# Linear attention block on one core: moving the first loads between two queues, cutting the crossbar transfer finer, and waiting for every store at the end

## The chip, the cores and the metric

The kernel runs on 1 core of one Trainium2 chip. The metric is device microseconds of one execution. Times of the kernel before: 99.91, 99.98 and 100.34 us, so a median of 99.98 us. The profiled execution is one of its own, 100.18 us in all, of which the profile covers a span of 98.5 us.

A core has five instruction streams. PE multiplies matrices (PEld is its weight load), DVE and ACT work elementwise, POOL is used for constants here, and SP issues transfers. Transfers are issued from SP and ACT in this kernel; each of the two feeds a queue of its own, q1 for SP and q10 for ACT in the profile, and both queues are worked off by the same 16 DMA engines.

## The reference

```
x (1, 2048, 640), wqkv (640, 1920), wo (640, 640), all bf16; 32 heads of 20 columns
qkv = x @ wqkv                      # q, k, v
phi(t) = where(t > 0, t + 1, exp(t)) + 1e-6
pq, pk = phi(q), phi(k)
kv  = sum over s of pk[s, d] * v[s, e]     # per head, 20 x 20
z   = sum over s of pk[s, d]
num = pq @ kv ;  den = pq . z + 1e-6
out = (num / den) @ wo
```

The sequence has 2048 rows, which the kernel walks in 16 tiles of 128 rows.

## The kernel before

The program is written out by hand for each engine. A small class `Plan` records every operation with what it reads and writes, and works out which semaphores it must wait for (`add`, lines 36 to 76); `emit` then writes each engine's list in the recorded order. Every DMA has a semaphore of its own. An engine's `known` table holds the semaphore values that its earlier waits imply, so that a wait which is implied already is left out.

**Stages.** First come the keys. For each of the 16 row tiles, ten matmuls (five blocks of 128 of the contraction, two halves of 320 columns) compute x @ Wk into two PSUM banks (`k_half`, L293); ACT and DVE then make phi of it (`k_phi`, L306 to L311). After that PE runs the x-by-phi(k) products (L317), the query tiles (L354), small products for kv and the folded output weights (L445, L472), the denominators (L544), and the output (L576), whose tiles are stored row tile by row tile. The order of these is spelled out in one string.

**How x gets to PE.** A matmul needs x transposed, in the buffer `xT`. For row tiles 2 to 15 the transposed form is fetched by transposing transfers on SP (`load_xT`, L189), here called the crossbar transfers; the list `XCH` says which rows each of them covers. Tiles 0 and 1 (`NPE = 2`) are loaded plain into `xn`, transposed by PE against an identity (`transpose_x`, L200), and copied from PSUM to `xT`: part 0, blocks 0 and 1, by DVE (L212), part 1, blocks 2 to 4, by ACT (L209). `xn_keys` names what a transposition has to wait for.

**The loads at the head** (`load_wk`). SP issues the left half of x tile 0, then blocks 0, 2 and 3 of Wk, then the five crossbar transfers, and then `load_rest`: the query weights, the remaining plain x tiles, and the other weights. ACT issues the right half of x tile 0, x tile 1, and blocks 1 and 4 of Wk. A block of Wk is 128 rows of 640 columns, 160 KB, as much as one tile of x.

**PE at the head** (L625 to L636). Before the data is there PE runs dummy matmuls on constants (`warm`, L283): five of 512 columns and one of 128. Then it transposes tile 0, runs one more dummy matmul of 512 columns, and follows this list, in which `k` stands for key matmuls (row tile, block of the contraction, and with a letter only one of the two halves) and `t` for a transposition of tile 1:

```
order = "k00a t1a k00b t1b k10 k01 k11 k02 k12 k03 k13 k04 k14"
```

**The end** (L730 to L734). After all engines' lists SP waits for the output stores. A store is skipped there if SP's `known` table says that an earlier wait implies it.

Of the kernel before, what the change touches and what calls it, by code (L numbers as in the profile page):

```python
# [84 lines left out]
def bass_standalone__linear_attn_block__prompt_kernel(nc, x, wqkv, wo, out):  # L85
# [5 lines left out]
    HALF = D // 2  # L91
# [9 lines left out]
    with contextlib.ExitStack() as ctx:  # L101
        es = ctx.enter_context

        def sb(name, cols, dt=BF16):
            return es(nc.sbuf_tensor(name, [128, cols], dt))

        xT = sb("xT", NC_ * S)
        xn = sb("xn", NT * D)
# [23 lines left out]
        ident = sb("ident", 128)  # L132
# [7 lines left out]
        P = Plan(nc, es)  # L140

        def bank(b, n=BK, off=0, parts=128):
            return ps[0:parts, BK * b + off:BK * b + off + n]
# [9 lines left out]
        def pool_const():  # L153
# [21 lines left out]
            for t in range(2):  # L175
# [3 lines left out]

        NPE = 2  # L180
        XCH = [(0, 128), (128, 256),
               (256, 384), (384, 640), (640, 1024), (1024, 1536), (1536, 2048)]

        def xch_of(row):
            return next(i for i, (a, b) in enumerate(XCH) if a <= row < b)
# [7 lines left out]
        def transpose_x(st, part):  # L193
            lo, hi = ((0, 2), (2, NC_))[part]
            b = (6, 4)[st] + part
            v = bank(b, HALF).bitcast(BF16)

            def mm(e):
                for c in range(lo, hi):
                    r = e.transpose(  # L200
                        v[:, 128 * c:128 * c + 128],
                        xn[:, st * D + 128 * c:st * D + 128 * c + 128], ident[:, :])
                return r
            P.add("pe", mm, reads=xn_keys(st)[:1 + part] + ["ident"], writes=[("bank", b)])
            dst = xT[:, :].rearrange("p (c s) -> p c s", s=S)[
                :, lo:hi, 128 * st:128 * st + 128]
            src = v.rearrange("p (c s) -> p c s", s=128)[:, lo:hi, :]
            if part:
                P.add("act", lambda e: e.copy(dst, src),  # L209
                      reads=[("bank", b), "table"], writes=[("xT", st, lo)])  # L210
            else:
                P.add("dve", lambda e: e.tensor_copy(dst, src),  # L212
                      reads=[("bank", b)], writes=[("xT", st, lo)])
# [15 lines left out]
        def load_xn(a, b, eng):  # L229
            P.add(eng, lambda e: e.dma_start(  # L230
                xn[:, a * D:b * D].rearrange("p (t n) -> p t n", n=D),
                x[0, 128 * a:128 * b, :].rearrange("(t p) n -> p t n", p=128)),
                writes=[("xn", t) for t in range(a, b)], dma=True)

        def load_wk():
            tl = mybir.InstLoadActFuncSet(
                name=nc.get_next_instruction_name(),
                act_func_set_id=ACT_TABLE_SET_LN_EXP, ins=[], outs=[])
            P.add("act", lambda e: e.add_instruction(tl), writes=["table"])
            for eng, lo in (("sp", 0), ("act", HALF)):  # L240
                P.add(eng, lambda e, lo=lo: e.dma_start(  # L241
                    xn[:, lo:lo + HALF], x[0, 0:128, lo:lo + HALF]),
                    writes=[("xn", 0, lo)], dma=True)
            for eng, what in (("sp", "w01 w23 w34"), ("act", "x12 w12 w45")):
                for k in what.split():
                    a, b = int(k[1]), int(k[2])
                    if k[0] == "x":
                        load_xn(a, b, eng)
                    else:
                        P.add(eng, lambda e, a=a, b=b: e.dma_start(  # L250
                            wk[:, a * D:b * D].rearrange("p (c n) -> p c n", n=D),
                            wqkv[128 * a:128 * b, D:2 * D].rearrange("(c p) n -> p c n", p=128)),
                            writes=[("wk", c) for c in range(a, b)], dma=True)

        def xn_keys(t):
            return [("xn", t)] if t else [("xn", 0, 0), ("xn", 0, HALF)]

        def load_rest():
            w_cols(wqn, 0, D, 0, "wqn", "sp")
# [21 lines left out]
        def warm(n, cols=BK):  # L281
            for _ in range(n):
                P.add("pe", lambda e: e.matmul(  # L283
                    bank(4, cols), nc.const_aps.tensor(1.0, [128, 128], BF16),
                    nc.const_aps.tensor(1.0, [128, cols], BF16), start=True, stop=True),
                    writes=[("bank", 4)])
# [37 lines left out]
        def p_step(h, st, ds=range(NC_)):  # L324

            def mm(e):
                for d in ds:
                    r = state_mm(e, h, d, st)
                return r
            P.add("pe", mm, reads=xn_keys(st) + [("pk", st)],  # L330
                  writes=sorted({("bank", d // PB[h]) for d in ds}))
# [288 lines left out]

        pool_const()
        load_wk()
        load_xT()
        load_rest()
        warm(5)  # L625
        warm(1, 128)
        for part in range(2):
            transpose_x(0, part)
        warm(1)
        order = "k00a t1a k00b t1b k10 k01 k11 k02 k12 k03 k13 k04 k14"  # L630
        for k in order.split():
            st, part = int(k[1]), "ab".find(k[-1])
            if k[0] == "t":
                transpose_x(st, part)
            else:
                for h in range(2) if part < 0 else (part,):  # L636
                    k_half(st, h, (int(k[2]),))
# [41 lines left out]
        def p_block(h, ds):  # L679
            def mm(e):  # L680
                for d in ds:
                    for st in range(NB, NT):
                        r = state_mm(e, h, d, st)
                return r
            P.add("pe", mm, reads=[k for st in range(NB, NT) for k in xn_keys(st) + [("pk", st)]],
                  writes=[("bank", ds[0] // PB[h])])
            p_out(h, ds)
            if ds[-1] == NC_ - 1:
                small.extend((0, 1) if h else (2, 3, 4))
# [39 lines left out]
            P.emit(name, eng)  # L729
        for key in out_keys:  # L730
            op = P.writers[key]
            if P.known["sp"].get(op.sem, 0) >= op.val:
                continue
            nc.sync.wait_ge(P.sem_obj[op.sem], op.val)  # L734


# [26 lines left out]
```

## Time and profile before

| | |
|---|---|
| median of 3 runs | 99.98 us (99.91 to 100.34) |
| profiled execution | 100.18 us, span 98.5 us |
| PE busy | 97% of the span, 699 matmuls |
| DVE, ACT, POOL busy | 65%, 50%, 5% |
| first key matmul | 4.37 us after the span's start |
| first key matmul of row tile 2 | 7.9 us |
| last matmul's copy out of PSUM starts | 96.5 us |

Of each transfer at the head, the issue and the moment when all of it had landed (us from the start of the span):

| queue | transfer | issued | landed |
|---|---|---|---|
| SP | x tile 0, left half, 80 KB | 0.79 | 2.86 |
| SP | Wk block 0, 160 KB | 1.24 | 4.32 |
| SP | Wk block 2 | 1.70 | 5.18 |
| SP | Wk block 3 | 2.17 | 6.03 |
| ACT | x tile 0, right half, 80 KB | 0.82 | 3.03 |
| ACT | x tile 1, 160 KB | 1.24 | 4.51 |
| ACT | Wk block 1 | 1.72 | 5.36 |
| ACT | Wk block 4 | 2.21 | 6.23 |
| SP | crossbar, rows 256 to 384 | 2.65 | 7.02 |
| SP | crossbar, rows 384 to 640 | 4.03 | 9.02 |
| SP | crossbar, rows 640 to 1024 | 6.29 | 12.11 |
| SP | crossbar, rows 1024 to 1536 | 8.04 | 16.11 |
| SP | crossbar, rows 1536 to 2048 | 12.63 | 18.23 |

The profile's chain of work that ended last is followed back from the last instruction: where an instruction waited, the chain steps to what released it, and otherwise to the instruction before it on the same engine. The length of a piece is the time that it adds to the span. A matmul's duration in the profile is modelled and overlaps with the next one's; how far apart matmuls *start* is what a row of them costs.

### The profile page before, as it was taken

What the parts mean: (1) busy time and instruction counts of PE and PEld (TensorE: products, weight loads), DVE (VectorE), ACT (ScalarE), POOL (GpSimd) and SP (SyncE); (2) the same over time, 40 slices, a digit from 0 to 9 for tenths busy, and PEclk for the clock granted to TensorE, in tenths of its full rate; (3) what the DMA queues carried; (4) which work ended last, traced back from release to release, by engine and by line L of the source; (5) the groups of instructions that cost most, each with busy time, mean ns of one, the idle gap of its engine ahead of it and who ended that gap; (6) DMA issues with size and microseconds to landing.
All of it is one profiled execution on the core that took longest, in us unless ns stands there. A gap on an engine that the chain in (4) does not pass through costs nothing.

```text
span 98.5 us, 1813 instructions
## 1 busy us (share of the span) xinstructions
PE 95.4 (97%) x699; PEld 61.1 (62%) x699; DVE 63.7 (65%) x124; ACT 48.8 (50%) x93; POOL 4.7 (5%) x19
## 2 busy tenths in 40 slices
PE   6999999999999999999999999999999999999991
PEld 2567677777755454445587867655557677777771
DVE  5315988988899529997829836758999207272122
ACT  5116455544526220005806466796988765453532
POOL 6400000000000000000000420000000000000000
DMA  2999999999999177000250023313200335632334
GB/s 69 310 258 164 148 222 187 248 379 370 338 163 136 14 169 166 0 0 0 57 83 7 0 61 92 96 29 87 82 0 0 133 72 156 212 122 88 130 133 133
DMA packets 26367, 12.59 MB, mean 128 GB/s; under 512 B 18552, under 2 KB 26360, under 8 KB 26360
## 3 DMA queue, kind: packets, MB, share of 16 engines
q1 hardware_dynamic: 25640, 11.87, 50.3%
q10 hardware_dynamic: 720, 0.61, 1.9%
q8 instruction: 5, 0.08, 0.3%
q14 instruction: 2, 0.02, 0.1%
HBM read 5.90 MB, written 2.62 MB: 87 GB/s over the span
## 4 chain that ended last, share of the span: by engine, by line
PE 93%; DMA 3%; SPq 0%; issue 0%; ACT 0%
PE ps L293 23%; PE ps L576 22%; PE ps L317 22%; PE ps L354 22%; DMA wk<-in_wqkv_dram 3%; PE ps L445 1%; PE ps L544 1%; PE ps L472 1%; SPq L241 0%; PE ps L200 0%; ACT osb L599 0%
## 5 line engine op out<-in xcount | busy, mean ns | idle before, releaser
L317 PE MATMUL ps<-pk,xn 128*128 128x480 bf16 (+1 forms) x160 | 23.2, 299 | 0.0
L354 PE MATMUL ps<-xT,wqn 128*128 128x512 bf16 x100 | 23.1, 379 | 0.0
L293 PE MATMUL ps<-wk,xT 128*128 128x320 bf16 x160 | 22.6, 301 | 0.3 <-DMA wk<-in_wqkv_dram 0.2
L576 PE MATMUL ps<-w2p,pq 128*128 128x320 bf16 (+2 forms) x170 | 22.1, 291 | 0.0
L293 PEld LDWEIGHTS ps<-wk,xT 128*128 128x128 bf16 x160 | 15.5, 98 | 7.2 <-DMA wk<-in_wqkv_dram 0.8
L576 PEld LDWEIGHTS ps<-w2p,pq 128*128 128x128 bf16 x170 | 15.9, 98 | 6.2 <-issue 0.2
L317 PEld LDWEIGHTS ps<-pk,xn 128*128 128x128 bf16 x160 | 13.6, 98 | 9.4 <-issue 0.3
L362 ACT ACTIVATE eq<-ps 128x512 bf16<-128x512 f32 x20 | 11.9, 597 | 13.8 <-PE ps L354 13.6
L354 PEld LDWEIGHTS ps<-xT,wqn 128*128 128x128 bf16 x100 | 11.5, 118 | 9.1 <-issue 0.3
L306 ACT ACTIVATE ek<-ps 128x640 bf16<-128x640 f32 x16 | 11.2, 704 | 11.0 <-PE ps L293 10.3
L599 ACT CAST osb<-ps 128x320 bf16<-128x320 f32 (+2 forms) x27 | 11.0, 413 | 9.7 <-PE ps L576 8.8
L311 DVE SCALAR_TENSOR_TENSOR pk<-ps,ek 128x640 bf16<-128x640 f32 x16 | 13.2, 825 | 0.6
L569 DVE TENSOR_TENSOR pq<-pq,rd 128x512 bf16<-128x512 bf16 x20 | 7.3, 418 | 4.3 <-DMA rd<-rdc 4.3
L375 DVE TENSOR_SCALAR eq<-eq 128x512 bf16<-128x512 bf16 x20 | 5.7, 287 | 5.9 <-ACT eq L362 5.8
L602 DVE CAST osb<-ps 128x320 bf16<-128x320 f32 (+1 forms) x7 | 3.2, 455 | 8.7 <-PE ps L576 8.7
L308 DVE TENSOR_SCALAR ek<-ek 128x640 bf16<-128x640 bf16 x16 | 5.2, 325 | 5.3 <-ACT ek L306 5.3
L366 ACT ACTIVATE rq<-ps 128x512 bf16<-128x512 f32 x13 | 7.7, 592 | 0.0
L339 ACT CAST pt<-ps 128x480 bf16<-128x480 f32 x4 | 2.3, 563 | 8.2 <-PE ps L317 8.1
L379 DVE TENSOR_TENSOR pq<-eq,rq 128x512 bf16<-128x512 bf16 x13 | 5.5, 425 | 1.1 <-ACT rq L366 0.7
L388 DVE TENSOR_TENSOR za<-pk 128x1280 f32<-128x1280 bf16 x4 | 5.8, 1483 | 0.0
L382 DVE SCALAR_TENSOR_TENSOR pq<-ps,eq 128x512 bf16<-128x512 f32 x7 | 4.8, 692 | 0.2
L388 DVE TENSOR_TENSOR za<-za 128x1280 f32<-128x1280 f32 x3 | 4.4, 1487 | 0.0
(37 smaller groups left out, 36.6 us busy)
## 6 DMA issues: line engine op xcount, KB each, us to landing
out_dram<-osb SPq DMA_DIRECT2D x15, 160.0 KB, 1.8
xn<-in_x_dram SPq DMA_DIRECT2D x2, 640.0 KB, 9.3
xn<-in_x_dram SPq DMA_DIRECT2D x1, 960.0 KB, 7.4
wqn<-in_wqkv_dram SPq DMA_DIRECT2D x1, 800.0 KB, 5.3
wv<-in_wqkv_dram SPq DMA_DIRECT2D x5, 150.0 KB, 4.6
wog<-in_wo_dram SPq DMA_DIRECT2D x2, 375.0 KB, 5.0
w2p<-w2g SPq DMA_DIRECT2D x10, 75.0 KB
rd<-rdc SPq DMA_DIRECT2D x8, 64.0 KB, 2.2
```

Of the source, the lines that this page charges most:

```text
L293: r = e.matmul(bank(b + h, HALF), xT[:, c * S + 128 * st:c * S + 128 * st + 128], wk[:, c * D + HALF * h:c * D + HALF * (h + 1)], start=(c ...
L306: P.add("act", lambda e: e.activation(fold(t[:, :]), two_banks(b), ACTF.Exp), reads=banks + ["table"], writes=[("ek", st % 3)])
L311: P.add("dve", lambda e: e.scalar_tensor_tensor(fold(pk[:, st * D:(st + 1) * D]), two_banks(b), 0.0, fold(t[:, :]), ALU.max, ALU.add), rea ...
L317: return e.matmul(bank(d // PB[h], PW[h], off=PW[h] * (d % PB[h])), xn[:, st * D + 128 * d:st * D + 128 * d + 128], pk[:, st * D + PO[h]:s ...
L354: r = e.matmul(bank(b), wqn[:, d * D:(d + 1) * D].rearrange("p (q c) -> p c q", c=NC_)[:, c, :], xT[:, d * S + BK * sbk:d * S + BK * (sbk ...
L362: P.add("act", lambda e: e.activation(t[:, :], bank(b), ACTF.Exp), reads=[("bank", b), "table"], writes=[("eq", i)])
L366: P.add("act", lambda e: e.activation(r[:, :], bank(b), ACTF.Relu), reads=[("bank", b), "table"], writes=[("rq", i)])
L375: P.add("dve", lambda e: e.tensor_scalar(t[:, :], t[:, :], 1.0, 1e-6, ALU.min, ALU.add), reads=[("eq", i)], writes=[("eq", i)])
L388: P.add("dve", lambda e: e.tensor_tensor(d_ap, a, b, ALU.add), reads=ra + rb, writes=[dst])
L569: P.add("dve", lambda e: e.tensor_tensor(v, v, rd[i][:, BK * h:BK * (h + 1)], ALU.mult), reads=[("rd", i, 2 * h), ("rd", i, 2 * h + 1), (" ...
L576: r = e.matmul(bank(b, hi - lo), pq[:, c * S + 128 * st:c * S + 128 * st + 128], w2p[:, c * D + lo:c * D + hi], start=(c == 0), stop=(c == ...
L599: P.add("act", lambda e: e.copy(osb[j][:, lo:hi], bank(b, hi - lo)), reads=[("bank", b)], writes=keys)
```

## The change

Five edits, all at the head but for the last:

1. x tile 0 and x tile 1 are each loaded whole on SP, ahead of the crossbar transfers; both transpositions of tile 0 now wait for the whole tile.
2. Wk is loaded on ACT alone, in three transfers: blocks 0 and 1 (320 KB), blocks 2 and 3 (320 KB), block 4 (160 KB).
3. The crossbar transfers cover 128, 128, 256, 384, 384 and 512 rows (six) in place of 128, 256, 384, 512 and 512 (five).
4. The last of the dummy matmuls ahead of the first transposition has 256 columns, not 128, and the list of key matmuls at the head has another order: four key matmuls of tile 0 stand among the transpositions of tile 1, where two stood.
5. At the end SP waits for every output store, also for those that an earlier wait implies.

```diff
         XCH = [(0, 128), (128, 256),
-               (256, 384), (384, 640), (640, 1024), (1024, 1536), (1536, 2048)]
+               (256, 384), (384, 512), (512, 768), (768, 1152), (1152, 1536), (1536, 2048)]
...
-            P.add("pe", mm, reads=xn_keys(st)[:1 + part] + ["ident"], writes=[("bank", b)])
+            P.add("pe", mm, reads=xn_keys(st) + ["ident"], writes=[("bank", b)])
...
-            for eng, lo in (("sp", 0), ("act", HALF)):
-                P.add(eng, lambda e, lo=lo: e.dma_start(
-                    xn[:, lo:lo + HALF], x[0, 0:128, lo:lo + HALF]),
-                    writes=[("xn", 0, lo)], dma=True)
-            for eng, what in (("sp", "w01 w23 w34"), ("act", "x12 w12 w45")):
+            for eng, what in (("sp", "x01 x12"), ("act", "w02 w24 w45")):
                 for k in what.split():
...
         def xn_keys(t):
-            return [("xn", t)] if t else [("xn", 0, 0), ("xn", 0, HALF)]
+            return [("xn", t)]
...
         warm(5)
-        warm(1, 128)
+        warm(1, 256)
         for part in range(2):
             transpose_x(0, part)
         warm(1)
-        order = "k00a t1a k00b t1b k10 k01 k11 k02 k12 k03 k13 k04 k14"
+        order = "k00 k01a t1a k01b t1b k10 k11 k02 k12 k03 k13 k04 k14"
...
         for key in out_keys:
             op = P.writers[key]
-            if P.known["sp"].get(op.sem, 0) >= op.val:
-                continue
             nc.sync.wait_ge(P.sem_obj[op.sem], op.val)
```

On the other engines, and from row tile 2 on, the order of instructions is the same as before. SP's wait list at the end grows from three instructions, which hold five semaphores, to nine instructions, which hold seventeen.

## The prediction

> **What bounds the kernel now.** I read the page first, then the chain that ended last, then the head, transfer by transfer, and last SP's waits. The page says which engine to think about:
>
> ```profile
> span 98.5 us, 1813 instructions
> PE 95.4 (97%) x699; PEld 61.1 (62%) x699; DVE 63.7 (65%) x124; ACT 48.8 (50%) x93; POOL 4.7 (5%) x19
> ```
>
> 97% busy says little by itself, because dummy matmuls count too. The chain shows where time can be had (start, length, what):
>
> ```profile
> 0.79 0.39 SPq L241
> 1.18 0.06 issue
> 1.24 3.09 DMA wk<-in_wqkv_dram
> 4.32 0.05 issue
> 4.37 0.45 PE ps L293
> 4.82 0.21 PE ps L200 x2
> 5.03 0.18 PE ps L293
> 5.22 0.17 PE ps L200 x3
> 5.38 0.04 issue
> 5.42 6.69 PE ps L293 x48
> 12.11 0.05 issue
> 12.16 15.12 PE ps L293 x110
> ...
> 96.51 0.02 issue
> 96.53 0.23 ACT osb L599
> ```
>
> From 4.37 us to 96.5 us it is PE without a break worth the name, and ahead of that one transfer of Wk. The first of the two small "issue" pieces, at 5.38, is the wait for DVE's copy of tile 1's transposed x. The other, at 12.11, is a wait for a crossbar transfer. Single starts in the timeline give its full size: key matmuls start 0.136 us apart, but one at 11.81 is followed by one at 12.16, so 0.35 - 0.136 = 0.21 us are lost, and the transfer for rows 640 to 1024 landed at 12.11. Behind the key stage no gap between starts is over 0.1 us. So whatever the change does ahead of row tile 2 (start 7.875) shifts the whole end by as much, and only two things can be won: part of the head, and those 0.21 us.
>
> **Edit 5, the waits at the end.** SP issues its last store at 96.54 (0.33 us), the last two stores land at 98.27 and 98.44, and SP's list of waits ends with the span. The twelve added semaphores stand in the list ahead of the pairs that hold the last two stores. Nine instructions instead of three, at 0.047 us each (on SP a wait that was met already starts that long ahead of the next instruction, 96.494 to 96.541), are 0.3 us more, between 96.87 and 98.2, where SP does nothing but wait:
>
> ```profile
> SPq L734 <- DMA out_dram<-osb: 1.4, 2, 0.8
> ```
>
> Cost 0. Without that cover, in a list that ended with the twelve, it would be 0.3 us. Nothing stands behind SP there.
>
> **Edits 1 and 2, the loads.** The same 1120 KB (two tiles of x, five blocks of Wk) are moved, in 5 transfers instead of 8, which costs nothing by itself: the issues lie beside PE's dummies. The first key matmuls used to need Wk block 0, which landed at 4.32. Now they need a 320 KB transfer which lies behind nothing on ACT's queue, but shares the engines with x tiles 0 and 1 on SP's. The DMA view of the first 4.2 us says how much had come by then, and that both queues had been served about evenly:
>
> ```profile
> DMA packets 709, 0.66 MB, mean 157 GB/s; under 512 B 67, under 2 KB 709, under 8 KB 709
> q1 hardware_dynamic: 390, 0.37, 32.6%
> q10 hardware_dynamic: 319, 0.29, 22.0%
> ```
>
> x tile 0, x tile 1 and blocks 0 and 1 of Wk are 640 KB, or 0.655 MB: with even service all of it has moved by 4.2. A transfer lands later than that, because its 16 shares do not end together: 0.49 MB (x 0, block 0, x 1) had moved at 3.7 and was landed at 4.51; 0.82 MB at 4.65, landed at 5.36. That is a lag of 0.7 to 0.8. So Wk blocks 0 and 1 land at 4.2 + 0.75 = 4.95, where block 0 alone landed at 4.32. Bounds: if ACT's queue is served ahead of x tile 1, the 0.49 MB row holds, 4.5; if the slow patch at 2.7 to 3.0 us (the DMA engines are under 7 tenths busy there) lasts twice as long, 5.3. I take 4.95, since the two queues' rows are nearly equal.
>
> Does anything else hold the first key matmul longer? x tile 0 shares with as much of Wk, 0.33 MB, moved by 3.25, so it lands at about 3.85 (before: 2.86 and 3.03). Five transpositions at 0.107 end at 4.4, DVE's copy 0.75 after their start, 4.6, the 512-column dummy at 4.4 + 0.43 = 4.82. None is over 4.95. The 256-column dummy ends at 3.12 instead of 3.02, ahead of x tile 0 either way: cost 0, hidden in that wait.
>
> **Edit 4, the order.** From 4.95: three key matmuls (k00, k01a) at 0.136 are 0.41, then the two transpositions of t1a at 0.056, the second starting at 5.42. Before, k10 started 0.70 after that point (4.719 to 5.42, at the low clock; the transposition itself is 0.31 long there and 0.22 at the high one), so 0.61 now: 6.03. In that time k01b and t1b run (0.30), so PE idles 0.3 where it idled 0.2. Sixteen key matmuls remain, at 0.136: 2.17, and row tile 2 starts at 8.20. Before it was 7.875. **Loss 0.33**, of which the later start is 0.58 and the two more key matmuls that now run ahead of the wait give back 0.25.
>
> The next transfers in this stretch: Wk blocks 2 and 3, 0.33 MB, alternate with crossbar packets a fifth as large, so 0.39 MB from 4.2 at the 0.65 MB in 2 us which the DMA view has from 4.2 to 6.2: 5.4, landed 6.15; wanted by k02 at 6.03 + 4 x 0.136 = 6.57. Block 4: 0.6 later, 6.75, wanted at 7.66. Margins 0.4 and 0.9.
>
> **Edit 3, the crossbar.** Two issues of 0.46 us fewer stand ahead of them on SP, so they are issued from 1.70, not 2.65; but their data waits for the same bytes, so I claim no earlier landing. Straight lines between the landings of before (7.02, 9.02, 12.11, 16.11) give rows 512, 768, 1152 and 1536 at 8.0, 10.0, 13.1 and 16.1. Wanted, with tile 2 at 8.20 and 1.358 a tile: tile 2 at 8.20, tile 3 at 9.56, tile 4 at 10.9, tile 6 at 13.6, tile 9 at 17.7. Margins 0.5 at least, so the 0.21 go away. **Gain 0.21.** Bounds: one more transfer could cost as much as an SP issue of this kind, 1.33 us for 128 rows, on the later ones; 13.1 + 1.33 against 13.6 is a new stall of 0.8; the best is the 0.21. What SP does behind them has room: the query weights landed at 21.55 and are first read at 29.3.
>
> **Sum.** +0.33 - 0.21 + 0 = +0.12 us. On the profiled execution 100.18 becomes 100.30; against the median of 99.98, which it exceeds by 0.2, **100.1 us**. Differences under 0.5% (0.5 us) can't be told from no change here, so this is no change.
>
> **Rivals.**
> - *Wk lands early* (16%). ACT's queue holds nothing but Wk, and by its bound the first key matmul starts at 4.5. Then tile 2 starts at 7.75: -0.13 - 0.21, 99.65; with the 0.3 us of waiting for DVE's copy hidden too, 99.35. For it: the three issues on ACT start at once. Against: nearly equal rows of the two queues.
> - *The clock rises later* (11%), slower. The 512-column dummies start 0.427 us apart, 1.2 columns a ns, and from about 5.0 us on, 4.2 us after the first of them, key matmuls take 0.136 and not 0.267. Before, PE was idle for 0.4 us (3.98 to 4.37) ahead of that point. Now I expect 0.7 (3.12 to 3.85) and 0.1. If PE is not busy enough for the rise and needs as long again from 3.85, it comes at 8.0: eleven matmuls between 4.95 and 8.0 at 0.13 more, +1.5 us, 101.6. It decides from the point where the idle time counts; nothing in the rows of before says where that is.
> - *A large transfer or a crossbar block is late* (14%), slower. Wk blocks 2 and 3 at 7.0 instead of 6.15 cost 0.45; rows 768 to 1152 by the bound above 0.8. With 0.33 from the head: 100.7 to 101.0.
> - *The waits at the end are not hidden* (3%): 0.3 us more, 100.4.
>
> A rule of the Trainium skill speaks against the longer idle time ("TensorE: Matmul & The Clock Gate", Part 1, on the clock gate): PE's clock is set by how busy it was in windows of about 3.4 us that run freely, whatever the kernel does. By the row above the clock rises at 5.0 again and the sum stays at +0.12; by the rule a window that counts as idle costs half of 3.4 us, an estimate of +1.7 on top. The single rise in the trace neither shows nor excludes it; it bears on the chance of this rival, and not on its price.
>
> **Chances.** The forecast has 56%, its own range 99.8 to 100.4. Faster by over 0.5% is half of the first rival, 8%; slower by over 0.5% is the clock, the late transfer, and the end's waits together with a late head, 28%; the rest, 64%, is within. The range for 8 in 10 leaves out the clock and the best of the first rival: 99.55 to 100.95.
>
> **What would show it.** In the profile after: the first key matmul at 4.95 released by Wk's transfer, tile 2 at 8.2, no gap at 12.1, PE's starts at 0.136 from 5.0 on, and the span's end 1.9 us after SP's last store was issued. A first key matmul before 4.6, or starts of 0.267 after 5.2, makes the prediction wrong.

## The result and the profile after

The changed kernel takes 99.64 us in the median of 20 runs (99.33 to 100.07), the kernel before 100.13 us in the median of 20 (99.72 to 102.76). The ratio is 0.9954, with a 95% interval of 0.994 to 0.9969: about 0.46 us faster. An execution that took over 1.5% longer than the fastest of its kernel, as the one of 102.76 us did, is left out of the ratios and means here and below. The profiled execution took 99.49 us, with a span of 98.2.

The page after, its first lines:

```profile
span 98.2 us, 1813 instructions
PE 94.8 (97%) x694; PEld 61.1 (62%) x699; DVE 63.7 (65%) x124; ACT 48.8 (50%) x93; POOL 4.7 (5%) x19
```

Note what does not add up: the two spans differ by 0.25 us (98.48 and 98.23), the two profiled executions by 0.69 (100.18 and 99.49). The time that lies outside the span went from 1.70 to 1.26 us. It turned out that this is where the gain is, and that a span says less than it seems to.

Inside the span, the chain after (start, length, what), from its first transfer to the end of the key stage and on:

```profile
0.78 2.64 DMA xn<-in_x_dram
3.42 0.05 issue
3.47 0.71 PE ps L200 x5
4.18 0.43 PE ps L279
4.61 0.54 PE ps L289 x3
5.15 0.12 PE ps L200 x2
5.28 0.02 issue
5.30 0.30 DVE xT L212
5.60 0.05 issue
5.65 21.36 PE ps L289 x156
27.01 2.03 PE ps L313 x10
...
96.25 0.02 issue
96.28 0.23 ACT osb L595
```

The chain now begins with x tile 0, which landed at 3.42, and goes through the transpositions and the 512-column dummy. Wk blocks 0 and 1 landed at 4.28, but the first key matmul started only behind that dummy, at 4.40, so Wk is no longer on the chain. From 5.65 on the key stage has no break; the one at 12.11 is gone. Row tile 2 starts at 7.83 (before: 7.875).

The end, in two lines of the rows of L728, SP's waits: how many, their lengths in ns, and when the first and the last of them started. The first line is of the window from 96.6 to 97.0, the second of 97.4 to 98.3; between the two there is none.

```profile
L728 SPq EVENT_SEMAPHORE  x5: 17/28/28, 96.7 to 96.9; - x5
L728 SPq EVENT_SEMAPHORE  x4: 28/28/28, 97.4 to 98.2; - x4
```

In the trace the waits before that pause start 0.07 us apart, the fifth at 96.949, and the sixth at 97.433. The sixth is for two stores that had landed at 84.21 and 95.76. So SP stood still for 0.41 us for nothing that is in the program, ahead of its 80th instruction. The kernel before has only 78 instructions on SP.

### The profile page after: what moved, and what is told of

The parts are those of the page before. It is cut to its first block, busy times and chain, and to the rows that moved or that the text cites. A ratio compares the mean times of both kernels' runs of the same rounds, so it can differ in the third digit from the quotient of the medians.

```text
span 98.2 us, 1813 instructions
## 1 busy us (share of the span) xinstructions
PE 94.8 (97%) x694; PEld 61.1 (62%) x699; DVE 63.7 (65%) x124; ACT 48.8 (50%) x93; POOL 4.7 (5%) x19
## 4 chain that ended last, share of the span: by engine, by line
PE 92%; DMA 3%; ACT 2%; issue 1%; DVE 0%
PE ps L289 22%; PE ps L572 22%; PE ps L350 22%; PE ps L313 21%; DMA xn<-in_x_dram 3%; ACT w2g L479 2%; PE ps L441 1%; PE ps L540 1%; PE ps L468 1%; PE ps L200 1%; PE ps L279 0%; DVE xT L212 0%; ACT osb L595 0%
## 5 line engine op out<-in xcount | busy, mean ns | idle before, releaser
L350 PE MATMUL ps<-xT,wqn 128*128 128x512 bf16 x95 | 22.0, 379 | 0.4 <-issue 0.2
L302 ACT ACTIVATE ek<-ps 128x640 bf16<-128x640 f32 x16 | 11.2, 704 | 10.5 <-PE ps L289 9.9
```

The lines of the kernel that those rows point to most:

```text
L302: P.add("act", lambda e: e.activation(fold(t[:, :]), two_banks(b), ACTF.Exp), reads=banks + ["table"], writes=[("ek", st % 3)])
L350: r = e.matmul(bank(b), wqn[:, d * D:(d + 1) * D].rearrange("p (q c) -> p c q", c=NC_)[:, c, :], xT[:, d * S + BK * sbk:d * S + BK * (sbk ...
```

## The experiments

Theories as they were formed: *A*, the gain is in the crossbar wait at row tile 5 and the head, as the prediction's terms have it, and the end brings nothing; *B*, part of it is outside the span and comes with edit 5. After the first four runs: *C*, SP stands still once, at a fixed place in its instruction list, and what counts is whether that falls under a wait or at the very end; against it *D*, the early stores must be waited for, and *E*, only work at the end helps.

**Edit 5 alone** (`e1_waits_only`), the kernel before without the two lines that skip a store:

```diff
-            if P.known["sp"].get(op.sem, 0) >= op.val:
-                continue
```

> The kernel before with edit 5 alone: SP waits for all seventeen store semaphores at the end. Theory A (the gain lies in the crossbar wait at row tile 5, 0.25 us, and the head; the end costs and brings nothing): ratio 1.000, 0.998 to 1.002, the same 0.21 us gap at 11.8 to 12.2 us, time minus span unchanged. Theory B (part of the gain lies outside the profiled span, since the profiled execution before took 1.70 us more than its span and the one after 1.26): 0.2 to 0.4 us faster, ratio 0.996 to 0.998, time minus span near 1.3.

Measured: 0.9969 (0.9946 to 0.9992), time minus span 1.27 in the mean of 10 runs, sd 0.03. Theory B. The windows of its waits from 96.9 to 97.25 and from 97.65 to 98.6, with none between, show the same pause, at 97.2 to 97.7:

```profile
L732 SPq EVENT_SEMAPHORE  x4: 17/28/28, 97.0 to 97.2; - x4
L732 SPq EVENT_SEMAPHORE  x5: 28/28/28, 97.7 to 98.6; - x5
```

**Edit 3 alone** (`e2_blocks_only`), the six row ranges in `XCH`:

```diff
-               (256, 384), (384, 640), (640, 1024), (1024, 1536), (1536, 2048)]
+               (256, 384), (384, 512), (512, 768), (768, 1152), (1152, 1536), (1536, 2048)]
```

> The kernel before with edit 3 alone: six crossbar transfers instead of five. Theory A: the gap of 0.21 us ahead of row tile 5 goes, the head up to row tile 2 stays (7.88), ratio 0.998 (0.996 to 1.000), span 98.25. Rival (the gap went because the crossbar transfers start behind other transfers, so edits 1 and 2 are needed): the gap stays or moves to another tile, ratio 1.000.

Measured: 1.002 (0.9991 to 1.0048), so no gain. No gap at row tile 5 in its profile. But the time minus span is 1.79, 0.11 more than before, with one more instruction on SP, and the mean span of 12 runs is 98.49, the same as before.

**Edits 1, 2 and 4** (`e3_head_only`), the changed kernel with the old `XCH` and the old waits. Against the kernel before, two of its hunks:

```diff
-            for eng, what in (("sp", "w01 w23 w34"), ("act", "x12 w12 w45")):
+            for eng, what in (("sp", "x01 x12"), ("act", "w02 w24 w45")):
...
-        order = "k00a t1a k00b t1b k10 k01 k11 k02 k12 k03 k13 k04 k14"
+        order = "k00 k01a t1a k01b t1b k10 k11 k02 k12 k03 k13 k04 k14"
```

> The kernel before with edits 1, 2 and 4: x on SP, Wk on ACT in three transfers, the new order at the head, and the old five crossbar transfers. Theory A: first key matmul at 4.4, row tile 2 at 7.83, and the gap ahead of row tile 5 stays or grows to 0.3, since SP issues its first crossbar transfer at 3.07 and not at 2.65: ratio 0.999 (0.997 to 1.002). Rival (the new loads bring more in the mean over executions than the profiled pair shows, for the clock rises at another moment in each): ratio 0.997.

Measured: 1.0005 (0.998 to 1.0029). Wk blocks 0 and 1 landed at 4.43, the first key matmul started at 4.48, and there is no gap at row tile 5, although the blocks are coarse. But row tile 2 starts only at 8.26, because key matmuls and transpositions still started at the low clock's distances (0.267 us for key matmuls) until 5.7 us: the clock rose later in this execution.

**All but edit 5** (`e4_head_and_blocks`), against the changed kernel:

```diff
+            if P.known["sp"].get(op.sem, 0) >= op.val:
+                continue
             nc.sync.wait_ge(P.sem_obj[op.sem], op.val)
```

> The changed kernel without edit 5. Theory A: the same as the changed kernel, ratio 0.995 to 0.997, no gap at row tile 5, row tile 2 at 7.83. Theory B (edit 5 brings part of it): 0.2 to 0.4 us less gain, ratio 0.998 to 0.999, time minus span near 1.7.

Measured: 0.9981 (0.9956 to 1.0006), which includes no change; its mean span, 98.43, is that of the changed kernel (98.42). Time minus span is 1.43, between the two values: this kernel has one instruction fewer on SP than the kernel before. So outside the span edit 5 brings 0.15 us here and 0.41 on the kernel before: it does not add up with the other edits. The last table of this section shows why.

Its profiled span is 99.0, the longest of the first four experiments. Key matmuls per microsecond show why (window, its length, PE busy with the number of matmuls, PEld likewise, granted clock in the column headed PEclk, DMA share, GB/s; a few records can be missing):

```profile
5.00:6.00 1.00, 0.99 (x4) 0.15 (x1) 1.00 1.17 306
6.00:7.00 1.00, 0.88 (x6) 0.54 (x6) 1.00 1.24 241
7.00:8.00 1.00, 1.00 (x10) 0.73 (x8) 1.00 1.26 283
```

and of the changed kernel's profile, the same rows:

```profile
5.00:6.00 1.00, 0.75 (x6) 0.38 (x5) 1.00 1.24 275
6.00:7.00 1.00, 1.00 (x9) 0.71 (x8) 1.00 1.29 237
```

The column of the granted clock says 1.00 throughout, and is no help here; the count is. From 5 to 7 us there are 10 key matmuls in one execution and 15 in the other; both also run transpositions of tile 1 there. The clock rose at 6.9 us in the first and at 4.85 in the second.

**Twelve idle waits at the end** (`e5_pad_end`), the kernel before with

```diff
+        for i in range(12):
+            nc.sync.wait_ge(P.sem_obj[f"d:{i}"], 16)
```

ahead of its own waits. These are semaphores of the first loads.

> The kernel before with twelve waits added at the end of SP's list, ahead of the three old ones, on semaphores of loads at the head, which were met 90 us earlier; no store is waited for that was not waited for before. SP's list has 84 instructions instead of 78. Theory C (SP's stream is fetched in blocks, and with 83 or more instructions the fetch of the next block starts under the wait for the last store instead of after the span): time minus span 1.27 instead of 1.68, 0.4 us faster, ratio 0.996, three packets of kind instruction on q14 instead of two. Theory D (it is the early stores' semaphores that must be waited for): ratio 1.000, time minus span 1.68, two packets.

Measured: 0.995 (0.9921 to 0.9979), time minus span 1.27. Theory C: nothing that matters is waited for, and the gain is all there. D is out. The count of packets on q14 turned out to be no sign by itself: it is three here, as expected, but also three in `e4_head_and_blocks`, which has 77 instructions.

**The same twelve in mid-program** (`e6_pad_early`), where SP idles ahead of the z sums' transfers:

```diff
+            if op is self.pad_before:
+                for i in range(12):
+                    handle.wait_ge(self.sem_obj[f"d:{i}"], 16)
```

> The same twelve waits, but ahead of SP's first crossbar transfer of the z sums, at about 49 us, when SP is idle and all of them are met; the end is that of the kernel before. SP has 83 instructions. Theory C: as the last one, time minus span 1.27, ratio 0.996. Theory E (only work of SP at the very end helps, whatever it is): ratio 1.000 and time minus span 1.68.

Measured: 0.9967 (0.9944 to 0.999), time minus span 1.24. The program's end is that of the kernel before; the 80th instruction of SP now lies between two output stores, where SP has time. E is out.

**Four such waits at the end** (`e7_pad_two`), that is 80 instructions:

```diff
+        for i in range(4):
+            nc.sync.wait_ge(P.sem_obj[f"d:{i}"], 16)
```

> The kernel before with four such waits at the end, held by two more instructions: SP has 80. Theory C with the fetch at the 83rd instruction: no gain, time minus span 1.6 to 1.8, ratio 1.000, two packets on q14. If each instruction gave its share of the gain: a third of it, ratio 0.9987.

Measured: 0.9998 (0.9966 to 1.003), no gain, as theory C has it. But the time minus span is 1.31 and not 1.6 to 1.8: the pause has not gone, it now lies between SP's 79th and 80th instruction, the 80th being the last wait, and so inside the span, whose mean is 98.90 where the kernel before has 98.49. The rows of its waits from 98.4 on:

```profile
L736 SPq EVENT_SEMAPHORE  x2: 28/28/28, 98.4 to 98.9; - x2
```

In the trace these start at 98.422 and 98.898, 0.48 apart; the last two waits of the kernel before start at 98.284 and 98.453, 0.17 apart. A fetch of 8 KB of instructions follows the 80th instruction by 0.6 us in each of these traces (99.52 here, 98.09 in the changed kernel, 98.32 with edit 5 alone). That the pause is SP asking for this block is an inference from that order, not shown. In the kernel before such a fetch comes at 99.62, 1.1 us behind the span's end. The place that the expectations of these runs named, the 83rd instruction, was wrong; it is the 80th.

**Another order at the head** (`e8_order`), on the changed kernel, meant as a version better than both:

```diff
-        order = "k00 k01a t1a k01b t1b k10 k11 k02 k12 k03 k13 k04 k14"
+        order = "k00 t1a k01 t1b k10 k11 k02 k12 k03 k13 k04 k14"
```

> The changed kernel with the key matmuls at the head in the order k00 t1a k01 t1b k10 k11 and so on, so that tile 1's first transposition runs one key matmul earlier and the wait for DVE's copy (0.245 us in the profile after) is shorter by 0.136. Theory: 0.1 us faster than the changed kernel, ratio to the kernel before 0.994 to 0.995. Rival (the 0.1 us is smaller than what the clock's rise moves from one execution to the next, 0.8 us): not to be told from the changed kernel.

Measured: 0.996 (0.9929 to 0.9991). The wait ahead of k10 is 0.11 us instead of 0.245, as meant, but the time can't be told from the changed kernel.

**x tile 1 behind Wk on ACT** (`e9_x1_behind_wk`, one execution), to see in what order the queues are served:

```diff
-            for eng, what in (("sp", "x01 x12"), ("act", "w02 w24 w45")):
+            for eng, what in (("sp", "x01"), ("act", "w02 x12 w24 w45")):
```

> The changed kernel with x tile 1 issued on ACT behind Wk blocks 0 and 1, and not on SP; SP issues its first crossbar transfer right behind x tile 0, at about 1.3 us. Theory F (transfers are served in the order of their issue across the two queues, so that Wk blocks 0 and 1, issued second, need not share): Wk blocks 0 and 1 land at 4.3 to 4.6 as before, the crossbar transfer's packets start right behind them, at about 3.5, and x tile 1 and all that follows on ACT come later by it, Wk block 4 after 6.5. Rival G (as predicted: the queues are served evenly): the crossbar's packets start at 2.3 to 2.6, beside those of Wk, and Wk blocks 0 and 1 land at 4.6 or later.

Measured: theory F, in one execution. Wk blocks 0 and 1 landed at 4.42. SP issued its crossbar transfer at 1.24, but its packets started only at 3.8, behind those of the Wk transfer issued at 0.82. That is 2.55 us after the issue; the first transposing transfer of the z sums, issued at 48.05 when both queues were empty, sent its first packet after 1.19, so the delay is not the transfer's own. From 2.75 to 3.75 us the queues' lines are:

```profile
q10 hardware_dynamic: 282, 0.35, 95.1%
q1 hardware_dynamic: 39, 0.04, 10.2%
```

SP's 39 packets there are what was left of x tile 0. The order is not strict for transfers issued close together: x tile 1, issued on ACT 0.06 us behind the crossbar transfer, sent its first packet at 3.68, beside it. Behind that, the rest came late, as expected: x tile 1 at 4.97, Wk blocks 2 and 3 at 7.07, block 4 at 7.58, and PE waited 0.87 us for blocks 2 and 3, ahead of 7.11. The changed kernel from 2.6 to 3.5 us shows the same one-sidedness: x tile 1, issued at 1.23, sends nothing until Wk's transfer, issued at 0.80, is nearly through.

```profile
q10 hardware_dynamic: 199, 0.25, 83.5%
q1 hardware_dynamic: 22, 0.02, 7.0%
```

**Edits 3 and 5** (`e10_blocks_and_waits`), the kernel before with the two diffs of `e2_blocks_only` and `e1_waits_only`:

> The kernel before with edits 3 and 5: finer crossbar transfers and all waits at the end, with the old loads and the old order at the head. Theory C (SP stops for 0.4 us ahead of its 80th instruction, and edit 5 moves that under the wait for the last stores; edits 1 to 4 are worth under 0.2 us together): 0.4 to 0.5 us faster, ratio 0.9950 to 0.9965, time minus span 1.27, the same as the changed kernel within the intervals. Rival (the new loads carry some of the gain): 0.9970 or above.

Measured: 0.9978 (0.9953 to 1.0003), less than expected and not settled. The ratio falls where the rival has it, though the interval holds both. The time minus span is 1.26, as expected by theory C, but the mean span of 11 runs is 98.60. Its profiled execution, not one of the 11, has a span of 100.4, and the reason shows in the rows of the key matmuls:

```profile
5.00:6.00 1.00, 0.88 (x2) 0.21 (x2) 1.00 1.17 352
6.00:7.00 1.00, 0.99 (x4) 0.60 (x5) 1.00 1.14 204
7.00:8.00 1.00, 1.00 (x6) 0.58 (x4) 1.00 1.27 257
...
10.00:11.00 1.00, 1.00 (x10) 0.71 (x8) 1.00 1.28 291
```

The clock rose at 9.2 us: from 5 to 8 us there are 2 to 6 key matmuls per microsecond, and 10 only in the last row. Wk block 0 had landed at 4.92 instead of 4.32, so PE had idled for 1.0 us behind its dummies. Row tile 2 started at 10.02, 2.14 us later than in the kernel before, and the span is 1.94 longer; the gap of 0.21 at row tile 5 is not there.

**Edits 1, 2, 4 and 5** (`e11_head_and_waits`), the changed kernel with the old `XCH`:

> The changed kernel with the old five crossbar transfers, that is the kernel before with edits 1, 2, 4 and 5. Theory C: 0.4 us from the end, time minus span 1.27; the mean span shows what the head is worth without the finer blocks: 98.5, as the kernel before, if the 98.68 of the head alone was the clock's lottery; 98.7 if the new loads cost 0.2 us without finer blocks. Ratio 0.996 or 0.998.

Measured: 0.9963 (0.9938 to 0.9989), time minus span 1.26, mean span 98.49, where `e3_head_only`, with the same edits inside the span, had 98.68. The mean span of both together, 24 runs, is 0.10 us above that of the kernel before, with a 95% interval of 0.14 to either side: what the head alone costs can't be told from nothing.

**The kernel before once more** (`e12_before_again`, one execution; no edit):

> The kernel before once more, unchanged, for a second profile of the same program. Theory H (the moment at which PE's clock rises differs from one execution to the next, and moves the span with it): the rise at another moment than 5.05 us, anywhere between 4.5 and 7, row tile 2 later by up to half of the difference, and no 0.21 us gap at row tile 5 if the rise is late. Rival (the rise is fixed by the program): 5.0 to 5.1, span 98.5 and the gap of 0.21 again.

Measured: theory H in part. The clock rose at 4.90 instead of 5.05, and row tile 2 started at 7.72. The gap at row tile 5 was there again, 0.26 us (the crossbar transfer landed at 12.01), and the chain now runs through it:

```profile
PE 84%; DMA 6%; SPq 5%; ACT 2%; issue 1%
PE ps L576 22%; PE ps L354 22%; PE ps L317 21%; PE ps L293 15%; DMA xT<-in_x_dram 6%; SPq L189 3%; ACT w2g L483 2%; PE ps L445 1%; PE ps L544 1%; SPq L250 1%; PE ps L472 1%; SPq L241 0%; ACT osb L599 0%
```

All together, with SP's instructions, the means, and the ratio to the kernel before:

| kernel | SP instructions | time minus span, us | mean span, us | runs | ratio |
|---|---|---|---|---|---|
| edits 1, 2, 4 | 76 | 1.50 | 98.68 | 12 | 1.0005 |
| edits 1 to 4 | 77 | 1.43 | 98.43 | 12 | 0.9981 |
| before | 78 | 1.68 | 98.49 | 88 | 1 |
| edit 3 | 79 | 1.79 | 98.49 | 12 | 1.002 |
| before, two idle instructions | 80 | 1.31 | 98.90 | 12 | 0.9998 |
| edits 1, 2, 4, 5 | 82 | 1.26 | 98.49 | 12 | 0.9963 |
| after (all five) | 83 | 1.28 | 98.42 | 20 | 0.9954 |
| after, another order at the head | 83 | 1.28 | 98.57 | 12 | 0.996 |
| edit 5 | 84 | 1.27 | 98.54 | 10 | 0.9969 |
| before, idle waits at the end | 84 | 1.27 | 98.48 | 12 | 0.995 |
| before, idle waits in the middle | 84 | 1.24 | 98.60 | 12 | 0.9967 |
| edits 3 and 5 | 85 | 1.26 | 98.60 | 11 | 0.9978 |

From 82 instructions on the time outside the span is 1.24 to 1.28 whatever else is changed; below 80 it is 1.43 to 1.79.

Where the pause lies in the kernels with fewer than 80 instructions can be read from the traces too. Their records of semaphore updates go on behind the program's last instruction: about nine in ten of the semaphores 7 to 255 are written once more there, in five series of some 50 numbers each, side by side. Of two of these series, the times in us from the span's end:

| SP instructions | traces | first update of all | first of 156 to 206 | first of 207 to 255 |
|---|---|---|---|---|
| 76 | edits 1, 2, 4 | 0.15 | 0.33 | 0.69 |
| 77 | edits 1 to 4 | 0.13 | 0.32 | 0.82 |
| 78 | before (two traces) | 0.54 | 0.73 | 0.71 |
| 79 | edit 3 | 0.66 | 0.84 | 0.80 |
| 80 | before, two idle instructions | 0.17 | 0.36 | 0.31 |
| 82 to 85 | the other eight | 0.13 to 0.14 | 0.31 to 0.33 | 0.26 to 0.28 |

With 78 and 79 instructions everything behind the span comes 0.4 to 0.5 us later than with 80 or more: here is the pause that the kernel before pays for. With 76 and 77 only the series of 207 to 255 is late, by 0.4 and 0.55, while the others go on beside it, and only a part of that is in the time. That this series is SP's own share of the work behind the program is an inference.

No version beats the changed kernel clearly; the lowest ratio, 0.995 for the kernel before with idle waits, has an interval that holds the changed kernel's.

## Why the prediction was wrong

The forecast was no change, 100.1 us, in a range of 99.8 to 100.4, with 8% for a gain of over 0.5%. Measured are 99.64 us and a ratio of 0.9954, a gain of 0.46% whose interval leaves out no change. The wider range for 8 in 10, from 99.55, holds the measured time by luck: none of its terms is where the gain came from.

**The step that failed is "Edit 5, the waits at the end ... Cost 0".** The reasoning in it was right as far as it went: the twelve semaphores are met before the last stores land, and SP's last wait still ends with the last store. The span still ended 1.95 us after the last store was issued, where 1.9 was forecast. What it took for granted is "Nothing stands behind SP there", and so "100.18 becomes 100.30" with the 1.70 us outside the span carried over. SP pauses for 0.41 us ahead of its 80th instruction. In the kernel before that comes behind its 78th and last, with nothing to hide it: what follows the program starts 0.54 us behind the span's end, and 0.13 in the changed kernel. With 83 instructions the pause lies under the wait for the last stores. Edit 5 alone gives 0.9969, and waits that wait for nothing give the same. Of the 0.46 us, 0.40 is the time minus span (1.68 to 1.28).

**Edits 1 and 2: the sharing was wrong.** The prediction let both queues share evenly and had Wk blocks 0 and 1 at 4.95. The rows that it took this from could not show it: in the kernel before the two queues' transfers were issued in pairs (1.237 and 1.238 us, 1.699 and 1.722), so service in the order of issue looks even as well. Wk blocks 0 and 1 landed at 4.28, and at 4.33 to 4.58 in the four other profiles with these loads: x tile 1, issued later, did not share. That was the bound named with 4.5 ("if ACT's queue is served ahead of x tile 1"), though the cause is the order of issue rather than the queue. x tile 0 was put at 3.85 and landed at 3.42. The first key matmul started at 4.40, before the 4.6 that the prediction named as a sign against itself, and what held it last was the dummy matmul of 512 columns, whose end the prediction had at 4.82. So the later start, put at 0.58 us, was 0.03 in the two profiled executions (4.40 against 4.37).

**Edit 4** was priced well where its start was right: from first key matmul to k10 the profile has 1.25 us, the prediction 1.08; the difference is the low clock at its beginning.

**Edit 3: the mechanism was right in some executions only.** The gap at row tile 5 appears in two of eight profiles with the coarse blocks, the two of the kernel before, with the clock up at 4.90 and 5.05. In the other six, with the clock up between 5.09 and 6.47, the crossbar transfer had landed earlier, at 10.5 to 11.5 against 12.0 and 12.1, and in five of them PE was later too. So 0.21 to 0.26 is what it can give in an execution that has the gap, not what it gives in the mean; alone it gave 1.002.

**Sum of edits 1 to 4.** Predicted +0.12 us in the span. Measured, by the mean span of kernels with edits 1 to 4 (32 runs) against the kernel before (88 runs): 98.42 against 98.49, or -0.06 before rounding, with a 95% interval of about 0.12 to either side. So inside the span there is no change that can be told, as forecast, but +0.12 itself lies outside that interval. The two terms also were not independent. A head that is 0.33 us late would have row tile 5 wanted at 8.20 + 3 x 1.358 = 12.27, behind the landing at 12.11, so the gap would go without edit 3, and the new head alone would cost 0.12. It measured +0.10, with 0.14 to either side (24 runs). Edit 3 on the old head, where -0.21 was due, measured +0.06, with 0.18 to either side (23 runs). On the new head it measured -0.17, with 0.16 to either side (32 runs against 24), so a gain there isn't excluded, though no profile of the new head shows a gap that it could close.

**The rivals.** "Wk lands early" was the right rival for the head, and it gave 99.65 by its sum; that the measured 99.64 agrees with it is chance, since the head did not bring the 0.34 us. "The clock rises later" is real, but differs between single executions, and nothing ties it to the change: the rise came at 4.67 to 9.2 us in eight profiles with the old loads and at 4.72 to 6.86 in six with the new. "The waits at the end are not hidden" had the wrong sign.

## What to carry to other kernels

Take the time outside the profiled span as a quantity of its own: when it differs between two kernels, look at the instruction count of the queue that ends last, before explaining the gain by anything in the span. Adding waits that are met to a list under a long wait can be free, or better than free, and a change that adds or removes a transfer can move the end through its instructions alone: outside the span one instruction more cost 0.11 us here (edit 3), and six idle ones more brought 0.41. Where a head depends on a clock that rises at its own time, compare mean spans of many executions; two profiles differ by more than the edit.

## What the runs showed that was not expected

**The clock.** Read from the first key matmul or transposition that is followed at the high clock's distance, the rise came at 4.67 to 6.86 us in thirteen profiles and at 9.2 in one, with the first dummy matmul always at 0.8. Two executions of the very same program had 4.90 and 5.05. The span goes with it: 98.13 us at 4.67, 99.02 at 6.86, 100.42 at 9.2, about half a microsecond for each microsecond. That is rough, since these are three different kernels. The Trainium skill, "TensorE: Matmul & The Clock Gate", Part 1, has the clock follow PE's activity in free-running windows of some 3.4 us; rises that spread over 2.2 us and one more that lies a further 2.3 us later, behind the longest idle stretch, fit such windows but do not show them. Idle time alone does not order the rises: behind 0.11 us of idle PE ahead of the first key matmul (four idle waits at the end) the clock rose at 6.47, behind 0.39 us (the kernel before) at 5.05.

**The order of service.** Two queues on the same engines did not take turns. A transfer's packets start when most of those of the transfers issued before it, on either queue, have been sent: in the changed kernel x tile 0 (issued 0.78) from 1.8 us, Wk blocks 0 and 1 (0.80) from 2.4, x tile 1 (1.23) from 3.5, Wk blocks 2 and 3 (1.29) from 4.0, the first crossbar transfer (1.69) from 5.1. The Trainium skill, "DMA: Bandwidth & Descriptors", "Queues, rings and completion order", has each engine alternate between the queues that have work for it. With 10% against 95% of the engines' time, that would mean that SP's queue had little work yet for the engines, although its crossbar transfer had been issued at 1.24; what the engines' queues hold is in no record here.
